# Two 1 KB inputs of a decode block issued from GpSimd instead of SyncE's queue

## The chip, the cores and the metric

One core of a Trainium2 chip runs the whole program; the other cores are idle. The metric is the device time of one execution in microseconds (us). A kernel before and a kernel to be compared are run on the same chip in the same rounds.

## The reference

One token is decoded through an adaptive-layer-norm block: a modulation vector from `silu(c) @ w_mod`, a layer norm of `x`, attention of 32 query heads over a cache of 8 K/V heads with 32768 positions, an output projection, a second layer norm and a ReLU feed-forward layer. Cut to what matters:

```python
mod = (silu(c) @ w_mod)                      # c: 512 values, w_mod: 512 x 3072
sa, ca, ga, sb, cb, gb = split(mod, 6)
h = layernorm(x) * (1 + ca) + sa             # x: 512 values
q = h @ wq                                   # 512 x 4096
scores = q . k_cache ; p = softmax(scores) ; o = p . v_cache    # 8 heads x 32768 x 128 each
x = x + ga * (o @ wo)
h = layernorm(x) * (1 + cb) + sb
x = x + gb * (relu(h @ w1) @ w2)
```

The two caches are 67 MB each in bf16; all inputs together are 149.4 MB. `c` and `x` are 1 KB each, and nothing after them can be computed without them.

## The kernel before: the parts that matter

All big inputs go through one queue, SyncE's, in a fixed order, into a ring of four slots of 4 MB. A load that reuses a slot waits on SyncE until the slot's reader is done. `need` issues loads up to the one asked for.

```python
def stream_dma(dst, src):
    i = nc.sync.dma_start(out=dst, in_=src)
    ...
stream = [("wm",), ("wq",)] + [("k", 0, (2 * G, 2 * G + 1)) for G in range(NG)]
...                              # then K of head g+1 and V of head g in turns, wo, w1, w2
wm_sb = need(("wm",))
cx_row = const.tile([16, D // 8], BF16)
stream_dma(cx_row[0:8], c[0].rearrange("(a n) -> a n", a=8))
stream_dma(cx_row[8:16], A_x[0, 0].rearrange("(a n) -> a n", a=8))

ident_bf = const.tile([P, P], BF16)
make_identity(nc, ident_bf[:])               # GpSimd
ident_f = const.tile([P, P], F32)
make_identity(nc, ident_f[:])                # GpSimd
...                                          # VectorE: four "sel" copies, then small masks from the identities
qbd = [const.tile([P, 4, 8, P], BF16, name=f"qbd{i}") for i in range(2)]
nc.gpsimd.memset(qbd[0][:], 0.0)
nc.gpsimd.memset(qbd[1][:], 0.0)
...
nc.vector.tensor_tensor(out=cx_bd[:], in0=cx_row[...], in1=pick8[...], op=ALU.mult)   # first use of c and x
```

From `cx_bd` a chain of small steps, called "the front" here, leads over silu, `mod`, the layer norm, `q` and `qbd` (the queries spread out as a stationary operand) to the first scores. VectorE transposes each K tile (`KTt`), PE multiplies (`S_ps`). A K slot comes free when its transposes are done; a V slot when PE's product with it is. Below, K1 is the first K load of the second head (the first that has to wait for a slot, `w_mod`'s), and V0 is the first V load (it takes the slot of `wq`, so it waits for the product that makes `q`).

## Time and profile before

| | kernel before |
|---|---|
| time, median of the first three runs | 355.64 us (355.63 to 355.8) |
| span of the profiled run | 353.7 us |
| one queue's share of the 16 DMA engines | 98.4% |
| bytes through it | 149.43 MB |
| PE busy / VectorE busy | 79% / 59% |

The profile's page and its views are read in the prediction below, with their lines. Two things help in reading them. A row of digits is a row of 40 slices of the span, each digit the busy tenths of a slice. And "from issue to landing" runs from the instruction that issues a load until the semaphore says that its data is there, so it contains all older loads that the queue still had to move.

### The profile page before, as it was taken

What the parts mean: (1) busy time and instruction counts of PE and PEld (TensorE: products, weight loads), DVE (VectorE), ACT (ScalarE), POOL (GpSimd) and SP (SyncE); (2) the same over time, 40 slices, a digit from 0 to 9 for tenths busy, and PEclk for the clock granted to TensorE, in tenths of its full rate; (3) what the DMA queues carried; (4) which work ended last, traced back from release to release, by engine and by line L of the source; (5) the groups of instructions that cost most, each with busy time, mean ns of one, the idle gap of its engine ahead of it and who ended that gap; (6) DMA issues with size and microseconds to landing.
All of it is one profiled execution on the core that took longest, in us unless ns stands there. A gap on an engine that the chain in (4) does not pass through costs nothing. (4 is left out here: it accounts for less than half of the span.)

```text
span 353.7 us, 4064 instructions
## 1 busy us (share of the span) xinstructions
PE 278.1 (79%) x1348; PEld 111.8 (32%) x1351; DVE 207.3 (59%) x269; ACT 28.2 (8%) x68; POOL 8.5 (2%) x14
## 2 busy tenths in 40 slices
PE   0352781999898979897969797979789787989995
PEld 0121230333343423332323233333333233334445
DVE  8555774882868268472949177553938095743050
ACT  1212004000110011001100101010100010020000
POOL 9000000000000000000000000000000000000000
PEclk9995997799899999999999998999999999999999
DMA  8999999999999999999999999999999999999994
GB/s 317 450 419 452 432 412 437 448 419 424 459 419 422 445 437 421 437 441 419 437 448 419 424 459 416 426 436 437 422 434 445 426 424 448 430 422 422 423 418 186
DMA packets 7076, 149.59 MB, mean 423 GB/s; under 512 B 792, under 2 KB 1048, under 8 KB 2200
## 3 DMA queue, kind: packets, MB, share of 16 engines
q1 hardware_dynamic: 7064, 149.43, 98.4%
q8 instruction: 8, 0.13, 0.1%
q14 instruction: 4, 0.03, 0.0%
HBM read 149.42 MB, written 0.00 MB: 422 GB/s over the span
## 5 line engine op out<-in xcount | busy, mean ns | idle before, releaser
L411 DVE STREAM_TRANSPOSE KTt<-Ksb 128x2048 f32<-128x2048 f32 x64 | 143.2, 2283 | 66.5 <-DMA Ksb<-in_A_k_cache_dram 58.8
L493 PE MATMUL o_ps<-Vsb,PT_g 128*16 (+1 forms) x512 | 128.0, 382 | 22.4 <-ACT qbd L395 9.5
L431 PE MATMUL S_ps<-KTt,qbd 128*128 128x512 bf16 x512 | 122.5, 391 | 22.2 <-DVE KTt L411 20.6
L431 PEld LDWEIGHTS <-qbd 128*128 128x128 bf16 x512 | 49.0, 98 | 87.0 <-issue 29.1
L493 PEld LDWEIGHTS o_ps<-Vsb,PT_g 128*16 x416 | 35.9, 86 | 90.7 <-issue 66.4
L437 DVE TENSOR_SCALAR_CACHE_REDUCE S_g<-S_ps 128x512 f32<-128x512 f32 x16 | 11.0, 690 | 27.7 <-PE S_ps L431 27.7
L395 ACT COPY qbd<-qrep_sb 32x128 bf16<-32x128 bf16 x32 | 9.4, 295 | 139.0 <-PE S_ps L431 137.9
L474 DVE STREAM_TRANSPOSE PT_g<-P_g 128x1024 bf16<-128x1024 bf16 x8 | 9.7, 1218 | 6.6 <-ACT P_g L468 6.6
L465 ACT ACTIVATE nbias<-Mb_ps 128x1 f32<-128x1 f32 x8 | 1.4, 171 | 131.1 <-PE Mb_ps L463 131.1
L493 PEld LDWEIGHTS <-PT_g 128*16 128x16 bf16 x96 | 8.2, 90 | 11.0
L233 PE MATMUL xc_ps<-cx_sel,cx_bd 16*128 16x2 bf16 x4 | 0.3, 172 | 12.8 <-DVE cx_bd L227 12.8
L468 ACT ACTIVATE P_g<-S_g,nbias 128x1024 bf16<-128x1024 f32 x8 | 9.2, 1148 | 0.2
L524 DVE SCALAR_TENSOR_TENSOR Y<-o_ps,smask,Y 16x128 f32<-16x128 f32 x24 | 8.1, 339 | 0.8
L179 DVE COPY sel<-ident_bf 128x128 bf16<-128x128 bf16 x4 | 7.6, 3730 | 0.0
L480 PE MATMUL L_ps<-Lexp,ones_f 128*128 128x4 f32 x16 | 3.0, 257 | 4.3 <-DVE Lexp L477 4.3
L606 PE MATMUL spare_ps<-qbd,ident_bf 128*128 128x512 bf16 x16 | 5.1, 380 | 0.2 <-issue 0.2
L449 PE MATMUL mT_ps<-ident_f,m_p 128*1 128x128 f32 x8 | 2.2, 270 | 3.9 <-DVE m_p L446 2.0
L452 DVE TENSOR_REDUCE Mrow<-mT_ps 1x4 f32<-1x128 f32 x8 | 2.1, 257 | 5.3 <-PE mT_ps L449 5.3
L480 PEld LDWEIGHTS L_ps<-Lexp,ones_f 128*128 128x128 f32 x16 | 3.1, 222 | 5.7 <-issue 5.1
L543 DVE TENSOR_TENSOR oT_sb<-acc_ps,Linv 128x4 bf16<-128x4 f32 x8 | 1.2, 151 | 5.7 <-PE acc_ps L530 5.7
L514 DVE MEMSET o_ps<- 16x512 f32 x8 | 3.9, 485 | 0.8
L561 DVE CAST o_sb<-o_ps 128x4 bf16<-128x4 f32 (+2 forms) x4 | 0.7, 166 | 6.1 <-PE o_ps L557 6.1
(112 smaller groups left out, 85.2 us busy)
## 6 DMA issues: line engine op xcount, KB each, us to landing
Ksb<-in_A_k_cache_dram SPq DMA_DIRECT2D x16, 4096.0 KB, 29.2
Vsb<-in_A_v_cache_dram SPq DMA_DIRECT2D x15, 4096.0 KB, 24.5
wq_sb<-in_A_wq_dram SPq DMA_DIRECT2D x1, 4096.0 KB, 18.8
Vsb<-in_A_v_cache_dram SPq DMA_DIRECT2D x2, 2048.0 KB, 23.4
wm_sb<-in_w_mod_dram SPq DMA_DIRECT2D x1, 3072.0 KB, 10.4
wo_sb<-in_A_wo_dram SPq DMA_DIRECT2D x1, 2048.0 KB, 25.1
w_sb<-in_B_w_dram SPq DMA_DIRECT2D x1, 1344.0 KB
wo_sb<-in_A_wo_dram SPq DMA_DIRECT2D x1, 1024.0 KB, 27.0
```

Source lines behind the costliest of these rows:

```text
L179: nc.vector.tensor_copy(out=sel[:, hp, :].rearrange("p (a c) -> p a c", a=4), in_=src)
L395: nc.scalar.copy(out=o, in_=i)
L411: t = nc.vector.transpose(out=KTt[:].bitcast(F32), in_=Ksb[:, 32 * half:32 * half + 32, :].rearrange("p j d -> p (j d)").bitcast(F32),)
L431: nc.tensor.matmul(S_ps_tiles[g], lhsT=qbd[g % 2][:, hp, s, :], rhs=KTv[:, 16 * sl:16 * sl + 16, h, :, par], start=(t4 == 0 and sl == 0 an ...
L437: nc.vector.tensor_scalar(out=S_tiles[g][:, G, :], in0=S_ps_tiles[g], scalar1=1.0, scalar2=None, op0=ALU.mult, op1=ALU.max, accum_out=m_ti ...
L468: nc.scalar.activation(out=P_g[:], in_=S_g[:].rearrange("p g f -> p (g f)"), func=ACT.Exp, bias=nbias[:], scale=scale, accum_out=l_g[:],)
L474: nc.vector.transpose(out=PT_g[:], in_=P_g[:])
L480: nc.tensor.matmul(L_ps[:], lhsT=ones_f[:], rhs=Lexp[:], start=True, stop=True)
L493: nc.tensor.matmul(o_tiles[g][:], lhsT=PT, rhs=Vx, start=False, stop=False, skip_group_check=True)
L514: nc.vector.memset(o_tiles[g][:], 0.0)
L524: nc.vector.scalar_tensor_tensor(out=Y[:], in0=o[:, s], scalar=smask[:, s:s + 1], in1=Y[:], op0=ALU.mult, op1=ALU.add,)
L606: nc.tensor.matmul(spare[0], lhsT=ident_bf[:], rhs=qbd[0][:, 0, 0:4, :], start=True, stop=True)
```

## The change

The intent is to get `c` and `x` out of the queue behind 3 MB of `w_mod`: they are issued by GpSimd (the profile calls this queue `software_dynamic`), as its first instructions.

```diff
     wm_sb = need(("wm",))
     cx_row = const.tile([16, D // 8], BF16)
-    stream_dma(cx_row[0:8], c[0].rearrange("(a n) -> a n", a=8))
-    stream_dma(cx_row[8:16], A_x[0, 0].rearrange("(a n) -> a n", a=8))
+    nc.gpsimd.dma_start(out=cx_row[0:8], in_=c[0].rearrange("(a n) -> a n", a=8))
+    nc.gpsimd.dma_start(out=cx_row[8:16], in_=A_x[0, 0].rearrange("(a n) -> a n", a=8))
```

The compiler also reorders VectorE's, ScalarE's and PE's work in the front because of it: the layer norm's square root and reciprocal come later, silu sooner.

## The prediction

> **What bounds the kernel now.** I read the page from the top: first the slices over time (row 2), then the chain that ended last (row 4), then the DMA queue and the time each load takes to land, and only then the first 45 us, in which the change lies. The page first; the rows are the busy tenths of VectorE and GpSimd, the DMA share and the GB/s in 40 slices of 8.84 us, the queue's totals, and the chain:
>
> ```profile
> span 353.7 us, 4064 instructions
> ...
> DVE  8555774882868268472949177553938095743050
> ...
> POOL 9000000000000000000000000000000000000000
> ...
> DMA  8999999999999999999999999999999999999994
> ...
> q1 hardware_dynamic: 7064, 149.43, 98.4%
> ...
> DMA Vsb<-in_A_v_cache_dram 7%; DMA w_sb<-in_B_w_dram 5%; PE ffn_ps L742 1%; SPq L139 0%; DVE o_rows L747 0%; DVE o_bf L749 0%
> ```
>
> The reader is to see that the DMA row is 9 from the second slice to the last but one, that no compute engine is, and that the one queue holds 98.4% of the 16 engines' span. The chain that ended last is a transfer, then a transfer, then 2.4 us of matmuls and the output. This kernel is a stream of 149.43 MB; whatever does not move the stream's start, its rate or its 5 us after the last landing does not move the time. A check: the first stretch of 9 us moved 325 GB/s x 9 us = 2.9 MB, which takes 6.7 us at 435 GB/s (the ceiling that the skill states, below; the stretch from 36 to 340 us has 432), so data began at about 2.3 us; 149.43 MB at 435 GB/s are 343.5 us more, which gives 345.8 us; the last weights land at 348.3 us, and some 1.6 us of that is the lag between the last byte and the semaphore (below). The stream ran at its ceiling from start to end, with under 1 us lost in all.
>
> Is there a place where the stream could run dry? That is in the time from issue to landing, for the K and the V loads (the columns are minimum, median and maximum):
>
> ```profile
> DMA to landing us min/median/max: 23.2/29.2/38.0
> ```
>
> ```profile
> DMA to landing us min/median/max: 17.9/24.5/36.2
> ```
>
> A load of 4.19 MB moves in 9.6 us at 435 GB/s. The shortest K landing takes 23.2 us, so at every issue some 13 us of older work stood in the queue. The SyncE queue may be late by that much and no DMA engine notices.
>
> Now the start, as the timeline gives it (start, duration, engine, operation, and the idle time before it):
>
> ```profile
> 0.74 0.39 SPq L139 DMA_DIRECT2D wm_sb<-in_w_mod_dram  x1
> ...
> 1.19 0.37 SPq L139 DMA_DIRECT2D cx_row<-in_c_dram  x1
> ...
> 1.60 0.28 SPq L139 DMA_DIRECT2D cx_row<-in_A_x_dram  x1
> ...
> 1.89 7.61 DVE L179 COPY sel<-ident_bf 128x128 bf16<-128x128 bf16 x4
> 1.93 0.36 SPq L139 DMA_DIRECT2D wq_sb<-in_A_wq_dram  x1
> ...
> 5.21 3.51 POOL L182 MEMSET qbd<- 128x4096 bf16 x1
> ...
> 12.07 0.68 DVE L227 TENSOR_TENSOR cx_bd<-cx_row,pick 16x512 bf16<-16x512 bf16 x1
> ...
> 15.07 3.58 PE L301 MATMUL mod_ps<-wm_sb,siluT 128*1 128x512 bf16 x24 [0.79 <-DVE siluT L295]
> ...
> 27.36 0.10 PEld L431 LDWEIGHTS <-qbd 128*128 128x128 bf16 x1 [1.83 <-ACT qbd L395]
> 30.48 8.89 DVE L411 STREAM_TRANSPOSE KTt<-Ksb 128x2048 f32<-128x2048 f32 x4 [4.51 <-DMA Ksb<-in_A_k_cache_dram]
> 32.84 8.89 PE L431 MATMUL S_ps<-KTt,qbd 128*128 128x512 bf16 x32 [7.20 <-DVE KTt L411]
> ```
>
> Three things are to be seen. The first use of c and x, cx_bd at 12.07 us, has no idle time before it: VectorE came to it straight from its own work, so c and x were not what it waited for, although they stand in the queue behind the 3 MB of w_mod (landed at 0.74 + 10.4 = 11.1 us). VectorE's lateness is GpSimd's: its four copies take 7.61 us because they end only when GpSimd's two memsets of 3.51 us end at 8.72. And from cx_bd on the whole front ends in waits for data: VectorE sits 4.51 us before the first K arrives, and PE 7.20 us before the first transposed K. K's landing checks the stream again: w_mod, wq and the first K are 11.53 MB, 26.5 us from 2.3 is 28.8, and it lands at 30.48, the lag of 1.6 us.
>
> **What the Trainium skill says.** "DMA: Bandwidth & Descriptors", section "Issuing engines are not separate DMA queues": loads from any engine run on the same 16 DMA engines and interleave, and issuing from several engines only saves the issuing sequencer's time. The trace agrees as far as it can: SyncE's two issues take 0.37 and 0.28 us out of a queue that is 13 us ahead. The same page, "Specifications", puts the ceiling at 435 GB/s; the middle of this trace (36 to 340 us) has 432. The same page, "Latency and other measured facts", gives about 1 us to the first byte for GpSimd's software path against 0.6 us, owing to the emission of descriptors by its cores; no GpSimd load is in the kernel before, so the trace cannot say. "SBUF — State Buffer", section "Who interferes with whom", says that VectorE in a two-port mode and GpSimd exclude each other; the 7.61 us of copies that end with the memsets agree with it.
>
> **The change part by part.** *Removed*: two issues of SyncE, (1.93 - 1.19) = 0.74 us, so wq and the first two K loads are issued 0.74 us sooner. They stand behind 3.15 MB of w_mod, which take 7.2 us to move, so 0 us of it reaches the stream. From the ring go 2 KB. The whole stream of some 50 issues loses under 1 us against its ceiling, so two entries are worth 2 x 0.02 = 0.04 us as an estimate. *Added*: two issues at the head of GpSimd's queue, ahead of the identity matrices. As an estimate from the skill's 1 us each, GpSimd starts its memsets at 2.7 instead of 0.73 us, and all of its 8 us of set-up moves by about 2 us; I allow 1 to 3. c and x themselves land at about 4 us instead of 11, which nobody can use, as VectorE is then still at the copies. *Moved*: VectorE waits for the identity, so copies, reductions and cx_bd go from 12.07 to about 14.1 us. Between cx_bd and the first w_mod matmul the compiler's new order takes the statistics of the layer norm (the copy at 14.32 that waited 0.74 us for PE) out of the way of silu, which gives back about 0.7 us: mod starts at about 16.4, not 15.07. Later the order pays that back: the square root's table load (1.28 us) and the reciprocal now come after the mod rows are copied and after the two 0.5 us memsets of q_ps. I call it even: the queries are ready about 2 us late, so the first LDWEIGHTS of scores at 29.4 instead of 27.36. The slack to the matmul that waits for K is 32.84 - 27.36 = 5.5 us, and VectorE's own is 4.51 us; a shift of 2 fits, and 3 does. The buffers of w_mod and wq come free at about 20.5 and 26 us instead of 19 and 24, so K1 and V0 are issued that much later; the loads queued before them last until 2.3 + 15.7 MB / 435 GB/s = 38 us, so the queue has over 12 us in hand. On the path that sets the end: -0.04 us + 0 + 0. The sum is nil: 355.6 us.
>
> **The rivals.** (1) *A faster start*: c and x were late behind w_mod and all that follows moves up. Against it: cx_bd had no wait, and the path runs into a wait for K in any case; were it so, the time would still be 355.6. (2) *GpSimd's delay exceeds the slack*: if two software issues took over 4.5 us, or if VectorE's copies held GpSimd off its descriptors, the first scores would start late. For it: the front hangs on GpSimd. Against it: GpSimd issues before VectorE has its identity, so there is no copy to hold it off; and even a delay of 6 us would have to empty a queue with over 12 us in hand. It would make the first scores late, and the time still 355.6 to 356. (3) *The stream itself*: a second queue with 128 B rows disturbs the big one, or the c and x entries, which take only part of the engines, were what one slow engine carried. Either way some tenths: 355.3 to 356. (4) *Outside the span*: the time is 1.8 us longer than the span; a kernel that uses the software path for the first time may have more to prepare or to close. Nothing in the trace bears on it; I allow +1 us.
>
> **Range and chances.** Runs of before lie within 0.05%, 355.63 to 355.8, but chips and builds may differ by 0.3%, which is 1.07 us. Below, 1 us: 354.6. Above, 1 us and a little for rival 4: 356.8. Two per cent are 7.1 us: to gain them the stream would have to start before it can or beat its ceiling, 0.01; to lose them the queue would have to run dry for 7 us, after a delay of some 20 us, or the rate fall by 2%, 0.02. Within 2%: 0.97.
>
> **What would show it right or wrong.** Right: the DMA row still 9 throughout; the chain ending in V, weights and ffn matmuls; GpSimd's first memset of the identity at 2 to 4 us; cx_bd at 13 to 15 us without a wait for c or x; the mod matmuls at 15.5 to 17.5; and VectorE's first transpose still at 30.4 to 30.6 us behind a wait for K that has shrunk from 4.51 to about 2.5 us. Wrong: a slice in the DMA row under 9 between the ends, a transpose that begins after 31 us with another releaser than K, a stretch of 36 to 340 us below 430 GB/s, or a gap between time and span that is not 1.8 us.

## The result, and the profile after

The changed kernel took 355.42 us (median of 6 runs, 355.22 to 356.46), the kernel before 355.77 us (6 runs, 355.63 to 357.04). The ratio is 0.9988, with a 95% interval of 0.997 to 1.0006. Ratios here and below are the mean time of one kernel's runs over the mean of the other's in the same rounds, so they are not quite the ratio of the medians. The time did not change measurably.

The page of the changed kernel (the same rows as in the prediction, and a new queue):

```profile
span 353.6 us, 4077 instructions
...
DVE  7737684982858367572949177553938095743040
...
POOL 8200000000000000000000000000000000000000
...
DMA  8999999999999999999999999999999999999995
...
q1 hardware_dynamic: 7032, 149.43, 98.5%
...
q0 software_dynamic: 64, 0.00, 0.0%
...
DMA Vsb<-in_A_v_cache_dram 7%; DMA w_sb<-in_B_w_dram 5%; PE ffn_ps L742 1%; SPq L139 0%; DVE o_rows L747 0%; DVE o_bf L749 0%
```

The DMA row is as full as before, and the same chain ends last. Only VectorE's second to fourth slices and GpSimd's second differ by more than a tenth: GpSimd's work ends in the second slice. The timeline of the front (start, duration, engine, operation, idle time before it):

```profile
0.74 0.40 SPq L139 DMA_DIRECT2D wm_sb<-in_w_mod_dram  x1
...
1.25 0.65 POOL L163 DMA_DIRECT2D cx_row<-in_c_dram  x1 [0.80 <-POOLq L765]
...
1.89 0.52 POOL L164 DMA_DIRECT2D cx_row<-in_A_x_dram  x1
2.40 0.23 POOL masks.py:197 MEMSET ident_bf<- 128x128 bf16 x1
...
13.75 0.68 DVE L227 TENSOR_TENSOR cx_bd<-cx_row,pick 16x512 bf16<-16x512 bf16 x1
...
30.02 0.10 PEld L431 LDWEIGHTS <-qbd 128*128 128x128 bf16 x1 [1.83 <-ACT qbd L395]
30.40 6.70 DVE L411 STREAM_TRANSPOSE KTt<-Ksb 128x2048 f32<-128x2048 f32 x3 [1.77 <-DMA Ksb<-in_A_k_cache_dram]
32.76 3.57 PE L431 MATMUL S_ps<-KTt,qbd 128*128 128x512 bf16 x8 [4.46 <-DVE KTt L411]
```

The two issues put off GpSimd's first identity memset from 0.73 to 2.40 us, so by 1.67 us; `cx_bd` follows from 12.07 to 13.75 us, still with no wait for data; the queries are ready at 30.02 instead of 27.36 us (1.31 us of that is a `q` product that ran at a lower clock in this trace, see experiment 2). There the delay ends: the first transposes and the first scores start at 30.40 and 32.76 us (in the kernel before at 30.48 and 32.84 us), because they wait for K. VectorE's wait for K shrank from 4.51 to 1.77 us and took up the delay.

### The profile page after: what moved, and what is told of

Its sections match the earlier page's. It is cut to its first block, busy times and chain, and to the rows that moved or that the text cites. A ratio compares the mean times of both kernels' runs of the same rounds, so it can differ in the third digit from the quotient of the medians.

```text
span 353.6 us, 4077 instructions
## 1 busy us (share of the span) xinstructions
PE 281.0 (79%) x1351; PEld 113.2 (32%) x1351; DVE 208.0 (59%) x269; ACT 28.2 (8%) x68; POOL 9.7 (3%) x16
## 5 line engine op out<-in xcount | busy, mean ns | idle before, releaser
L493 PE MATMUL o_ps<-Vsb,PT_g 128*16 (+1 forms) x512 | 129.6, 391 | 21.6 <-ACT qbd L395 9.6
L493 PEld LDWEIGHTS o_ps<-Vsb,PT_g 128*16 x416 | 37.0, 89 | 90.3 <-issue 64.3
L606 PE MATMUL spare_ps<-qbd,ident_bf 128*128 128x512 bf16 x19 | 5.9, 380 | 0.0
L368 PE MATMUL q_ps<-wq_sb,hT 128*1 128x512 bf16 x32 | 3.5, 621 | 1.2 <-DVE hT L284 1.2
```

Of the source, the lines that this page charges most:

```text
L493: nc.tensor.matmul(o_tiles[g][:], lhsT=PT, rhs=Vx, start=False, stop=False, skip_group_check=True)
L606: nc.tensor.matmul(spare[0], lhsT=ident_bf[:], rhs=qbd[0][:, 0, 0:4, :], start=True, stop=True)
```

## The experiments

Twelve kernels ran. Each is the changed kernel with the edit shown, unless it says otherwise, and all gave correct results. "d" is how much later the first scores start than at the 32.84 us of the kernel before.

### 1. The changed kernel again

No edit.

> The changed kernel once more, unaltered, to see whether its 0.12% (interval 0.997 to 1.0006) is real. Theory (the load stream sets the end, and the front has slack): ratio to the kernel before 0.999 to 1.0005, within 0.4 us. Rival (taking c and x out of SyncE's ring really shortens the stream by a few tenths): ratio 0.9985 to 0.9995 with an interval that leaves 1 out.

Measured: ratio 1.0001 (0.9981 to 1.0022), 356.08 us in 6 runs (355.32 to 357.2) against 356.08 us. What the first comparison showed, 0.12%, did not come back. No gain from emptying the ring of two entries can be told from nothing; one of my estimated 0.04 us could not be seen in any case.

### 2. From ScalarE's queue

```diff
-    nc.gpsimd.dma_start(out=cx_row[0:8], ...)     # and the one for x
+    nc.scalar.dma_start(out=cx_row[0:8], ...)     # and the one for x
```

> c and x issued from ScalarE's hardware queue, out of SyncE's ring as well and with no work for GpSimd. Theory: same time, within 0.4 us of before; GpSimd's identity memset back at 0.73 us and the mod matmuls at 15.1 us or a little sooner. If the landing of c and x 7 to 8 us after issue comes from sharing the 16 engines with w_mod and not from the software path, they land late here too, 5 to 8 us after issue; if it is the software path, they land within about 3 us. Rival (out of the ring is a gain): as much faster as the changed kernel.

Measured: ratio 1.0002 (0.9985 to 1.0019). GpSimd's identity is back at 0.73 us, `cx_bd` at 12.08 us, and the `mod` product starts at 14.21 us, 0.86 us sooner than in the kernel before: that is what the compiler's new order gives silu. V0, which waits for the `q` product, is issued at 25.02 us, against 23.98 us before and 26.85 us in the changed kernel. The order is only a part of this: the `q` product starts at 22.07 us, against 21.71 us before, so the order costs 0.36 us here. In the changed kernel the product starts at 23.28 us, 1.57 us later than before, which is GpSimd's delay of 1.67 us and nothing for the order. The rest is the product itself: it took 2.22 us before, 2.92 us here and 3.53 us in the changed kernel. The trace of experiment 1, of the same kernel without an edit, shows that this is not the change; first the changed kernel, then experiment 1:

```profile
23.28 3.53 PE L368 MATMUL q_ps<-wq_sb,hT 128*1 128x512 bf16 x32 [1.18 <-DVE hT L284]
```

```profile
23.13 1.90 PE L368 MATMUL q_ps<-wq_sb,hT 128*1 128x512 bf16 x32 [1.18 <-DVE hT L284]
```

The granted PE clock from 24 to 26 us was 0.50 in the first and 1.00 in the second, where V0 was issued at 25.07 us and the queries were ready at 28.45 us. Why the clock differed no run here shows. When c and x landed is not to be had from this trace, so it doesn't tell the software path from the shared engines; experiment 4 does.

### 3. c and x first, in SyncE's queue

From the kernel before:

```diff
-    wm_sb = need(("wm",))
     cx_row = const.tile([16, D // 8], BF16)
     stream_dma(cx_row[0:8], ...)
     stream_dma(cx_row[8:16], ...)
+    wm_sb = need(("wm",))
```

> c and x stay in SyncE's queue but ahead of w_mod, so the first big load is issued about 0.8 us later (1.55 instead of 0.74 us). Theory (the stream's start moves the end one for one): 0.6 to 0.9 us slower than before, ratio about 1.002, although c and x now land within about 3 us. Rival (the front's latency counts): faster or the same.

Measured: ratio 1.0016 (0.9999 to 1.0034), 356.6 us against 356.08 us. `w_mod` is issued at 1.50 us instead of 0.74. The size, 0.5 us, is just under what was expected, and the interval just holds 1, so this alone is not proof; the next one has the larger dose.

### 4. The stream held back, c and x on GpSimd with the engines free

```diff
     cx_row = const.tile([16, D // 8], BF16)
     nc.gpsimd.dma_start(out=cx_row[0:8], ...)     # and the one for x
+    junk_rows = const.tile([8, 6, D // 8], BF16, name="junk_rows")
+    for i in range(6):
+        stream_dma(junk_rows[:, i, :], c[0].rearrange("(a n) -> a n", a=8))
+    wm_sb = need(("wm",))
```

> The changed kernel with six loads of 1 KB that nobody reads put ahead of w_mod in SyncE's queue: the first big load is issued about 2.5 us later, while GpSimd's c and x go out at 1.25 and 1.89 us as before. Theory: 2.2 to 2.8 us slower, ratio about 1.007 (the stream's start one for one), and c and x land within about 3 us of issue because no bulk load shares the engines yet. If the software path itself takes 7 us, they still land 7 to 8 us after issue. Rival (the front's latency counts and the stream has slack): under 1 us slower.

Measured: ratio 1.0055 (1.0038 to 1.0072), 357.92 us against 356.08 us, so 1.8 us slower; `w_mod` was issued at 2.86 us, 2.12 us later (the six loads took 2.07 us and not my 2.5, and the time fell short of the 2.2 to 2.8 us that I had expected). The last weights landed at 350.80 us in the trace, 2.5 us later than before. The stream's start moves the end nearly one for one. The loads of c and x show the other thing; first the changed kernel's rows of issues (the last number is us to landing), then the answer for the c and x tile in this run:

```profile
cx_row<-in_c_dram POOLq DMA_DIRECT2D x1, 1.0 KB, 7.0
cx_row<-in_A_x_dram POOLq DMA_DIRECT2D x1, 1.0 KB, 8.2
```

```profile
DMA to landing us min/median/max: 1.6/1.7/1.7
```

With the same two instructions at the same 1.25 and 1.89 us, c and x landed after 1.6 and 1.7 us when no bulk load shared the engines, and after 7.0 and 8.2 us when one did. The software path is quick; the company is what makes it slow. VectorE's copies, which the second rival feared, are not needed for it: in experiment 5 x took 8.2 us to land, though the last of these copies had ended at 9.50 us, before its issue at 9.68 us.

### 5. GpSimd's loads behind its other work

```diff
-    nc.gpsimd.dma_start(out=cx_row[0:8], ...)     # and the one for x, ahead of the identities
     ...
     nc.gpsimd.memset(hid_bd[:], 0.0)
+    nc.gpsimd.dma_start(out=cx_row[0:8], ...)     # and the one for x
```

> The changed kernel with GpSimd's two loads moved behind all of its set-up: the identity is back at 0.73 us, and c and x are issued at about 9 us and, if they land 7 to 8 us later as in the changed kernel, VectorE waits for them until about 17 us (3.5 us later than in the changed kernel). Theory (slack in front): the first transposes of K start 0 to 3 us late, K1 and V0 are issued at about 23 and 30 us, before the queue's 36.8 us (38.4 us of queued loads less 1.6 us of latency): same time, within 0.5 us. Rival (the front's latency counts): some 3 us slower than the changed kernel.

Measured: ratio 0.9991 (0.9956 to 1.0025). The timeline:

```profile
9.04 0.65 POOL L219 DMA_DIRECT2D cx_row<-in_c_dram  x1
9.68 0.52 POOL L220 DMA_DIRECT2D cx_row<-in_A_x_dram  x1
...
17.98 0.68 DVE L227 TENSOR_TENSOR cx_bd<-cx_row,pick 16x512 bf16<-16x512 bf16 x1 [5.87 <-DMA cx_row<-in_A_x_dram]
```

Now VectorE does wait for x, 5.87 us, and `cx_bd` is 5.9 us later than in the kernel before. The first scores start at 34.16 us, so d is 1.3 us, and the time is the same. A real wait for the two inputs, in the place where the change was aimed, costs nothing either.

### 6 to 8. GpSimd slowed: six, twelve and twenty memsets

The second identity is made a part of a larger tile that is cleared n times first, so that the front waits for GpSimd:

```diff
-    ident_f = const.tile([P, P], F32)
+    pad_f = const.tile([P, 2048], F32, name="pad_f")
+    ident_f = pad_f[:, 0:P]
+    for _ in range(n):                            # n = 6, 12, 20
+        nc.gpsimd.memset(pad_f[:], 0.0)
     make_identity(nc, ident_f[:])
```

> The changed kernel with six extra memsets on GpSimd that the second identity waits for: the front some 10 to 15 us later. Theory: time = 355.5 to 356 plus what the issue of K1 exceeds 36.8 us; K1 at 28 to 36 us here, so no change beyond 0.5 us although scores start about 10 us late. Rival (PE, which is busy 79% of the span, cannot make good what it loses in front): 3 to 10 us slower.

> Twelve such memsets; the compiler then also puts a transpose of K, which waits for its landing at 30.4 us, ahead of the front's work on VectorE. K1 is issued at 42 to 52 us as an estimate. Theory: the DMA share drops in the slices from about 38 us until that issue plus 1.6 us, and the time is longer by the issue of K1 less 36.8 us, so 5 to 15 us slower, one for one within 1.5 us. Rival (later work makes it good): under 3 us slower. Rival (PE cannot catch up): slower by more than the hole in the stream.

> Twenty such memsets, the front later still, K1 issued at 50 to 65 us as an estimate. Theory: longer than before by the issue of K1 less 36.8 us, 13 to 28 us, within 1.5 us of that formula. Rivals as for twelve.

Measured:

| | first scores at | d | K1 issued at | ratio (95%) | median less the kernel before's |
|---|---|---|---|---|---|
| six | 41.57 us | 8.7 us | 31.0 us | 1.0085 (1.0048 to 1.0122) | 3.3 us |
| twelve | 53.16 us | 20.3 us | 44.8 us | 1.0436 (1.0399 to 1.0473) | 16.1 us |
| twenty | 64.49 us | 31.7 us | 55.9 us | 1.0754 (1.071 to 1.0799) | 26.6 us |

All three miss my formula, which counted from the issue of K1: it gave 0, 8.0 and 19.1 us. The DMA and GB/s rows of the run with six, then of the run with twenty, show why:

```profile
DMA  8999999989899999999999999999999999999995
GB/s 311 448 436 436 421 445 426 421 352 410 353 462 414 432 440 418 408 458 421 418 458 412 451 429 410 459 417 440 436 418 454 421 434 440 418 454 401 428 417 200
```

```profile
DMA  8999019999399999999999999999999999999995
GB/s 323 442 437 441 10 45 396 439 431 424 141 372 398 441 417 424 427 441 436 441 437 437 415 420 441 441 438 433 434 417 430 437 437 436 437 437 405 429 420 216
```

A slice of the first is 8.9 us, so its two holes lie at 71.6 to 80.5 us and at 89.5 to 98.4 us, and not at 38 us where I had put the queue's end. In the second, the hole at the fifth and sixth slices is the one I had predicted, and the one at the eleventh is the one that I had missed. Taking 432 GB/s as full, the holes of the second (10, 45, 141 and 372 in slices of 9.52 us) come to 9.3 + 8.5 + 6.4 + 1.3 = 25.5 us, close to the 26.6 us measured. So the holes in the stream account for nearly the whole loss.

The load behind the first hole of the run with six was K, issued at 78.52 us:

```profile
DMA to landing us min/median/max: 11.9/11.9/11.9
```

A 4 MB load that comes to an empty queue lands in 11.9 us. With that as the zero, the lines from the kernel before can be read anew: its shortest V load took 17.9 us, and a look at single loads puts it at the issue of 80.96 us. The queue's smallest cover (the time that the issue could be later before the stream runs dry), of the loads whose landing the trace gives, is therefore about 17.9 - 11.9 = 6.0 us, at 81 us. The zero is itself not sure for a V load: in the runs with five, six, twelve and twenty, the V load next to a hole took 13.3 or 13.4 us, and none took less; with 13.3 the cover is 4.6 us. In the changed kernel that load has 17.7 us, so 5.8 us of cover, and the K load at 70.06 us has 19.1, so 7.2 us.

A note on these three: in all of them (and with five, below) VectorE also does two or more transposes of K ahead of the front's last work, which can add to the delay; with six, two of them, of 2.28 and 2.27 us, stand before the queries are ready. They are doses of d, whatever makes it, and not measurements of GpSimd.

### 9 and 10. Four and five memsets

The same edit with n = 4 and 5, to try the revised reading near its edge.

> After six memsets cost 3.3 us where I had expected nothing, the theory is revised: the cover of the queue is smallest not at the start but at the V load issued at 81 us (17.9 us from issue to landing in the kernel before, against the 11.9 us of a load that finds the queue empty: 6.0 us of cover), and a front that starts scores later by d delays that issue by d. Four memsets, with d of 2 to 4 us as an estimate (scores at 35 to 37 us instead of 32.8): no change beyond 0.5 us, the V load near 84 us landing in 14 to 16 us. Rival (any loss of PE time in front is paid at the end): slower by d.

> Five memsets, d of 5 to 7 us as an estimate. Revised theory: at the edge, 0 to 1.5 us slower; the K load near 76 us and the V load near 87 us land in 12 to 14 us. Rival: slower by d, 5 to 7 us.

Measured, four: scores at 36.77 us, d 3.9 us; ratio 1.0028 (0.9993 to 1.0063), 356.77 us (355.48 to 358.02) against 355.9 us. That is 0.9 us more by the medians, just outside the half microsecond that I allowed, and unclear by the interval. The DMA row is full throughout. The V load, issued at 85.86 us, took 13.6 us, a little under the 14 to 16 that I expected.

Measured, five: scores at 39.83 us, d 7.0 us; ratio 1.0074 (1.0055 to 1.0092), 358.74 us against 355.9 us, so 2.8 us more, over the 1.5 I had allowed. The K load at 78.11 us took 12.0 us and the V load at 89.71 us 13.4 us, as expected. The issue of that K load moved by 8.1 us and not by d = 7.0 (70.06 to 78.11 us), which is part of the excess: PE does not keep the distance exactly.

With the others, the six doses make one line:

| d, us | 1.3 | 3.9 | 7.0 | 8.7 | 20.3 | 31.7 |
|---|---|---|---|---|---|---|
| slower by, us (medians) | 0.1 | 0.9 | 2.8 | 3.3 | 16.1 | 26.6 |
| d - 5, not under 0 | 0 | 0 | 2.0 | 3.7 | 15.3 | 26.7 |
| V load of 80.96 us issued later by, us | 2.3 | 4.9 | 8.8 | 8.7 | 21.9 | 32.1 |
| that less the cover of 6.0, not under 0 | 0 | 0 | 2.8 | 2.7 | 15.9 | 26.1 |

The third row is fitted by eye: about 5 us of delay of the first scores are free, and what exceeds it is paid one for one, within 1 us. The last row needs no fit: it counts the delay at the issue of the tightest load, which moved by up to 1.8 us more than d, and is within 0.9 us too. With the cover of 4.6 us it would be off by up to 1.4 us, so the free delay at that issue lies at 4.6 to 6.0 us, and the runs don't fix it better. The rival, that any loss of PE time in front is paid at the end, would have the second row equal to the first; at 7.0 and 8.7 us it is off by over 4.

### 11 and 12. The end of the kernel

Between runs the times lie from 355.2 to 357.2 us, and in the traces of experiments 1, 3 and 5 the chain that ended last was not of transfers but of PE's work. Two edits try the tail. In the one, the 1 before the last product becomes 17, in the other no clock-keeping matmul is left:

```diff
-        keep_clock(1)
+        keep_clock(17)

-        for _ in range(n):                        # in keep_clock
+        for _ in range(0 * n):
```

> The changed kernel with 16 more matmuls that nobody reads, after the last hidden activation and ahead of the second weight product; a pair of them takes 0.6 us and one more about 0.21 us, so some 3.4 us of PE. In the changed kernel PE waited only 0.16 us there for the last weights to land. Theory (PE and the stream arrive together at the end): 2.8 to 3.4 us slower, ratio 1.008 to 1.0095. Rival (only the stream counts, PE has over 2 us in hand there): under 1 us slower.

> The changed kernel without any of the matmuls that only keep the clock up in the tail. If PE arriving late at the end is what spreads the runs from 355.2 to 357 us, a shorter PE tail makes the time smaller and tighter, up to 0.5 us below the changed kernel and still bound by the last landing at 348.3 us; if the missing matmuls lower the granted clock, the tail gets longer by 1 us or more. The stream alone: no change within 0.3 us.

Measured, more: ratio 1.0068 (1.0052 to 1.0083), 358.44 us against 355.96 us, so 2.5 us slower for matmuls that take 3.61 us in the trace. It is less than the 2.8 to 3.4 that I expected, and far over the rival's 1 us: PE has about 1 us in hand at the end, no more. Measured, lean: ratio 1.0027 (1.0013 to 1.0042), 1 us slower. The last product in the changed kernel, in two parts, and in the lean one:

```profile
347.24 1.05 PE L742 MATMUL ffn_ps<-w_sb,hid_bd 128*4 128x128 bf16 x16 [0.23 <-ACT hid_bd L728]
348.45 2.39 PE L742 MATMUL ffn_ps<-w_sb,hid_bd 128*4 128x128 bf16 x40 [0.16 <-DMA w_sb<-in_B_w_dram]
```

```profile
347.22 5.46 PE L742 MATMUL ffn_ps<-w_sb,hid_bd 128*4 128x128 bf16 x56 [0.68 <-DMA w_sb<-in_B_w_dram]
```

In the changed kernel PE waits 0.16 us for the last weights: it and the stream arrive together. Without the spare matmuls the granted clock from 340 to 348 us is 0.60 instead of 1.00, and the same 56 matmuls take 5.46 us instead of about 3.6. The Trainium skill, "TensorE: Matmul & The Clock Gate", section "What's actually happening", says that an idle PE falls to half its clock. PE was not idle here but busy for 5.06 of the 8 us, and the mean of 0.60 lies between the half and the full clock; how long a pause it takes, this run doesn't show. So the tail could not be shortened in this way, and whether late PE is what spreads the runs stays open: it ended some traces and not others, but no run here sets it.

No version tried beats the two kernels.

## Why the prediction was right, and where a step of it was wrong

The time was right: 355.42 us measured for 355.6 predicted, and no change that stands clear of the noise. By its steps:

- *The bound.* Right. Holding the stream back by 2.1 us cost 1.8 us (experiment 4), and every hole in it cost its length (6 to 8). One sentence went too far: that whatever doesn't move the stream's start, its rate or the 5 us after it does not move the time. At the end PE has at most about 1 us in hand (experiment 11, and 0.16 us in the trace after), and in three other traces its chain ended last, so the bound there is shared.
- *Removed.* The 0.04 us for two ring entries can't be told from 0 (1.0001 in experiment 1).
- *Added.* GpSimd's delay was 1.67 us for an estimate of 2. That c and x would land at about 4 us was wrong: 7.0 and 8.2 us after issue put them at 8.3 and 10.1 us. They would have landed so only with the engines free (experiment 4). Nobody needed them before 13.75 us, so it cost nothing.
- *Moved.* `cx_bd` at 13.75 us for 14.1, `mod` at 15.89 us for 16.4, the queries at 30.02 us for 29.4. The new order was even to within 0.4 us up to the start of the `q` product, as I had called it. What the prediction left out is the PE clock of that stage: the product took 3.53 us in this trace and 1.90 us in another of the same kernel (experiment 2), so the queries came at 30.02 or 28.45 us and the wait for K was 1.77 or 3.60 us, for a forecast of about 2.5. That 29.4 lay near one of them is in part luck. All of it ended in that wait. One reading of the lines was loose: VectorE's copies end at 1.89 + 7.61 = 9.50 us, 0.78 us after the memsets' end at 8.72 and not with it; no run here separates the two engines there.
- *The queue in hand.* Wrong in size. The prediction held that over 12 us stood in the queue, by taking the K loads' shortest landing and the loads queued at the start, though the V loads' 17.9 us stood beside it; and it took off the 9.6 us of pure transfer, where a load that finds the queue empty needs 11.9. The tightest place is V at 81 us, with 4.6 to 6.0 us. So the sentence of the second rival that 6 us or more of delay would leave 355.6 to 356 us is refuted: 7.0 us of d cost 2.8 us and 8.7 us cost 3.3. The change was far from that edge, with d at -0.08 us.
- *The rivals.* That c and x were late behind `w_mod` is refuted twice: they had no waiter in the kernel before, and even a wait of 5.87 us for x left the time as it was (experiment 5). The gap between time and span did not grow: both profiled runs have 1.8 us (355.5 and 353.7 before, 355.37 and 353.6 after).

## What to carry to other kernels

Before moving a small load for its latency, look whether its first user has any idle time before it, and whether the path behind it runs into a wait for something else; here neither left anything to gain. To know how much delay a streaming kernel forgives, take the shortest time from issue to landing over all loads of the stream, for each kind of load, and take off what the same load needs on an empty queue: what is left is the slack at that load's issue (here 4.6 to 6.0 us), and beyond it every microsecond is paid. And a load moved to an otherwise idle engine is not free when other engines wait for that engine's next instructions.

## What the Trainium skill lacked or had wrong

- "DMA: Bandwidth & Descriptors", "Latency and other measured facts": its figure for the first byte of the software path, about 1 us, is not contradicted by a load with the engines free (landing 1.6 to 1.7 us after issue), but the page has none for a small load beside a bulk stream, which landed after 7.0 and 8.2 us. The section "Queues, rings and completion order" says that an engine takes turns between its queues packet by packet, from which one would hope for less; it also says that a semaphore's increment lands only after all earlier writes of that engine, which may be the reason, but no run here shows it.
- The same page, "Issuing engines are not separate DMA queues": what a plain 1 KB load costs the issuing GpSimd is missing; it was 0.65 and 0.52 us, and 1.67 us until the work behind the two began.
- The same page, "Where 436 GB/s comes from", says that loads from HBM are bound at about 358 GB/s; with the other cores idle this kernel moved 432 GB/s from 36 to 340 us, where the page's own single-core table has 425 GB/s at 16 MB.
- No page tells how to read a queue's slack from a profile: shortest landing 17.9 us less 11.9 us (13.3 us for the least of the V loads) gave 6.0 us (4.6 us), and delays of the first scores beyond about 5 us were paid.
